# Top-k attention with an MLP mixer on one core: another way to the 32nd largest score, output products in three pieces, other priorities in the plan

## The chip, the cores and the metric

The kernel runs on one core of one Trainium2 chip. The metric is device time in microseconds (us) of one execution, lower is better. A core has five engines that run their own instruction streams and meet at semaphores: PE (matmul), DVE (vector), ACT (activation), POOL (a second elementwise engine) and SP (here it only issues DMAs). All data that the engines work on lies in 128 partitions of on-chip memory; matmul results land in eight PSUM banks.

## The reference

Eight batches, eight heads, 576 rows, head size 64. Each row of scores keeps its 32 largest, and those below are masked; then comes softmax, the product with v, and an MLP mixer over tokens (576 to 256 to 576) and channels (512 to 1536 to 512).

```
scores = scale * np.matmul(q, k.transpose(0, 1, 3, 2))
kth = np.partition(scores, -top_k, axis=-1)[..., -top_k:-top_k + 1]   # top_k = 32
scores = np.where(scores >= kth, scores, -1000000000.0)
attn = np.exp(scores - np.max(scores, axis=-1, keepdims=True))
attn = attn / (np.sum(attn, axis=-1, keepdims=True) + 1e-09)
x = (attn @ v), heads side by side                                     # 8 x 576 x 512
u = x + (np.maximum(x^T @ w_tok1, 0) @ w_tok2)^T
out = u + np.maximum(u @ w_ch1, 0) @ w_ch2
```

## The kernel before

**Units.** The work is cut into 32 units, a pair of heads each (`plan_unit`); four units make a batch, and after each batch come the MLP's channel steps (`plan_mlp`; `plan_mlp_last` for the last batch). A unit has nine row tiles of 128 x 576 scores: tiles 0 to 3 are group 0, tiles 4 to 8 group 1 (tile 8 holds the last 64 rows of both heads).

**From q and k to scores.** SP loads q, k and v (`load_one`); PE transposes q and k (`qk_tr`, L281; `qk_tail_tr`, L296), ACT evacuates them (L291, L304), PE multiplies (`s1_mm` L311, `s0_mm` L334, `st_mm` L353) and ACT copies the scores from PSUM to the tiles SS (L324, L344) and St (L366). There are four SS tiles, one for each group, so two units can be in flight.

**The selection, on DVE.** For each group DVE folds the 576 scores of a row into 288 larger halves of pairs (`upper`, L384), and POOL works out the smaller halves by integer adds (`both_bits` L390, `lower_bits` L399: left + right - larger). `split4` (L407, L411) folds the 288 twice more by max and min. `top_round` (L423, L426) takes the eight largest of growing prefixes of this list four times (MAX8 gives eight values in descending order; MATCH_REPLACE takes them out), and `low_round` (L432) takes the eight largest of the smaller halves. The 40 values lie side by side in A. The first 16 are taken as certain; the 32nd largest is the 16th largest, that is, the eighth smallest, of the next 23. `combine` gets it with MAX8 on negated values:

```
nc.vector.tensor_scalar_mul(X[:, 0:n, :], A[:, 0:n, NR : NA - 1], -1.0)      # L438
for i in range(n):
    nc.vector.max(K[:, i, :], X[:, i, :])                                    # L441
nc.vector.tensor_scalar_mul(kthall[:, c : c + n], K[:, 0:n, 7], -1.0)        # L443
```

The last value of the lists is kept for a test at the end (`keep_ends`, L449, POOL). If that test (L1093 to L1103) finds a row for which the shortened lists were not enough, a slow exact path computes everything again (`full_select`).

**Mask, softmax, product.** ACT takes the exponential (`expo`, L483) with the negated row maximum (`neg_max`, L469, POOL). Tiles 0, 1, 2, 4 and 5 ("turned") are masked first: `raise_kth` (L496, POOL) scales the threshold, ACT makes a large number of all that lies below it (`steep`, L502), POOL subtracts it from the scores (`sink`, L510), and after the exponential a DMA transposes the tile (`turn`, L515). The other tiles are transposed on PE together with their mask (`below_act` L526, `p_tr` L532 and L535, `p_ev` L555, `ptail_tr`, `ptail_ev`). `o_mm` (L601) multiplies with v and a column of ones; there is one PSUM bank O. `o_den` (L613, L614) takes two reciprocals on DVE, one of the four full tiles and one of the 64 rows of the fifth; `o_ev` (L624) scales on ACT.

**MLP.** `h1_mm`, `ut_mm` and their evacuations follow each unit, `h2_mm` (L689) with `h2_ev` (L702) makes the 1536 channels of a batch, and `out_mm` (L711, L715, L719) the output: five row tiles of 15 matmuls each, every tile one task of the plan, in one of the two banks mps. `out_ev` (L731) evacuates, `out_st` stores.

**The order.** Every engine runs its instructions in a written order. `Plan` makes it: each task has an engine, an assumed duration, a priority (100 for each unit, plus an offset; the lowest first), the tasks it needs, and buffers that it takes and gives back. `order` plays this through, and at each free moment starts the ready task with the lowest priority. Where PE is idle in that play, `spare` (L244) puts in matmuls without use that keep PE's clock up. A buffer comes free in the play when the task that releases it ends; for SS, A, nmax and kbig this is a task of no length on POOL with an early priority.

Of the kernel before, what the change touches and what calls it, by code (L numbers as in the profile page):

```python
# [11 lines left out]
LAG = {"PE": 0.11, "ACT": 0.15, "DVE": 0.12, "POOL": 0.06, "SP": 1.2, "DQ": 0.0, "SPQ": 0.0}  # L12
# [3 lines left out]
SPARE = 0.8  # L16
SPARE_US = 0.22
# [7 lines left out]
class Plan:  # L25
# [23 lines left out]
    def order(self):  # L49
# [10 lines left out]
        while left:  # L60
# [13 lines left out]
            for e in free:  # L74
# [14 lines left out]
                if best is not None:  # L89
                    ready[e].remove(best)  # L90
                    if e == "PE" and best.dur > 0.0:
                        at, r, i = min(
# [4 lines left out]
                        )  # L97
# [30 lines left out]
def kernel(  # L128
# [32 lines left out]
    NA = 40  # L161
    NR, NV, NL = 16, 24, 32
# [27 lines left out]
    mgp = pool("mgp", 1)  # L190
# [35 lines left out]
    kthall = const.tile([P, NU * NTILE], f32, tag="kthall")  # L226
    ends = const.tile([P, NU * NTILE, 4], f32, tag="ends")
# [6 lines left out]
    }  # L234
    ctr = {"vb": 0, "pb": 0, "tp": 0, "s0": 0, "O": 0, "mps": 0}
# [180 lines left out]
    def top_round(st, g, r):  # L416
# [5 lines left out]
        for i in range(n):  # L422
            nc.vector.max(A[:, i, 8 * r : 8 * r + 8], hx[:, i, 0:w])  # L423
        if r < 3:
            for i in range(n):
                nc.vector.match_replace(  # L426
                    hx[:, i, 0:w], A[:, i, 8 * r : 8 * r + 8], hx[:, i, 0:w], NEG
                )

    def low_round(st, g):  # L430
        for i in range(4 + g):
            nc.vector.max(st["A", g][:, i, NL:NA], st["lo"][:, i, :])  # L432

    def combine(st, g, u):
        n = 4 + g
        A = st["A", g]
        X = mgp.tile([P, NS, NA - 1 - NR], f32, name="X", tag="X")
        nc.vector.tensor_scalar_mul(X[:, 0:n, :], A[:, 0:n, NR : NA - 1], -1.0)  # L438
        K = mgp.tile([P, NS, 8], f32, name="K", tag="K")
        for i in range(n):  # L440
            nc.vector.max(K[:, i, :], X[:, i, :])  # L441
        c = u * NTILE + 4 * g
        nc.vector.tensor_scalar_mul(kthall[:, c : c + n], K[:, 0:n, 7], -1.0)  # L443
        st["kth", g] = c

    def keep_ends(st, g, u):
        n = 4 + g
        c = u * NTILE + 4 * g
        nc.gpsimd.tensor_copy(out=ends[:, c : c + n, :], in_=st["A", g][:, 0:n, 15:NA:8])  # L449

    def full_select(st, g, u):
        c = u * NTILE + 4 * g
        A = m8p.tile([P, NS, NA], f32, name="A", tag="A")
        R = lists["hi"][:, 0:2, :].rearrange("p a c -> p (a c)")
        for a, i in enumerate(gtiles(g)):
            cur = srow(st, i)
            for r in range(TOPK // 8):
                nc.vector.max(A[:, a, 8 * r : 8 * r + 8], cur)
                if r + 1 < TOPK // 8:
                    nc.vector.match_replace(R, A[:, a, 8 * r : 8 * r + 8], cur, NEG)  # L460
# [727 lines left out]
```

## Time and profile before

| | us |
|---|---|
| median of three runs (1004.16 to 1007.36) | 1005.12 |
| the profiled execution | 1006.08 |
| its span, first to last instruction | 1004.2 |
| busy in the span: PE / DVE / ACT / POOL | 935.5 / 894.6 / 853.5 / 727.9 |
| DVE's first selection instruction starts | 15.18 |
| last threshold (L443) | 943.53 |
| mean granted PE clock | 0.979 |

The busy times are unions on each engine. PE's contains the matmuls without use. The chain that ended last is not of help here: followed back, it stops at the last output copy, so the stages have to be read from stretches and timelines. A group's row gives the line, the engine, the operation, what it writes and reads, how often it runs, its busy time and the mean length of one in ns, and the idle time just before it with what ended it. Lengths of neighbouring instructions overlap by some hundredths of a us, so costs in a row of instructions are read from start to start.

### The profile page before, as it was taken

Reading aid. Unit: us, or ns where it says so; the run is one execution under the profiler, and the core shown is the slowest. Engines: PE = TensorE matmul, PEld = TensorE weight load, DVE = VectorE, ACT = ScalarE, POOL = GpSimd, SP = SyncE. Lnnn points to the kernel's source line nnn. Section 1 sums busy time; section 2 is a strip of 40 time slices with the busy share of each in tenths; the row PEclk is TensorE's granted clock in tenths of the full one; section 3 lists DMA queues with packets and bytes.
Section 4 is the critical chain, followed back from the end, with each engine's and each line's share of the span. In section 5 each row is a group of like instructions: output and inputs, shape, how many; then the busy total and the mean of one; then the engine's idle time right before and its main releaser. Section 6 shows DMA issues by size and latency. Waiting matters only on the chain. (4 is left out here: it accounts for less than half of the span.)

```text
span 1004.2 us, 22286 instructions
## 1 busy us (share of the span) xinstructions
PE 935.5 (93%) x7128; PEld 502.9 (50%) x7128; DVE 894.6 (89%) x4088; ACT 853.5 (85%) x1976; POOL 727.9 (72%) x598
## 2 busy tenths in 40 slices
PE   9889999899999999999999999899999999989995
PEld 6444444455555455454545455454545555444542
DVE  3999999997999979999799979999799997999801
ACT  5667898898999988998999989999899989999731
POOL 3888888886688858888598867888688885888400
PEclk9989899999999999999999999999999999999998
DMA  7454122133332233123322333232233333211201
GB/s 167 120 174 130 38 63 60 45 63 105 68 69 51 69 87 87 40 62 77 81 58 60 80 100 79 45 68 74 66 69 63 75 99 68 46 34 31 71 1 51
DMA packets 229741, 72.65 MB, mean 72 GB/s; under 512 B 222128, under 2 KB 222704, under 8 KB 229616
## 3 DMA queue, kind: packets, MB, share of 16 engines
q1 hardware_dynamic: 229616, 71.15, 29.8%
q8 instruction: 58, 0.95, 0.4%
q14 instruction: 67, 0.55, 0.2%
HBM read 35.78 MB, written 9.44 MB: 45 GB/s over the span
## 5 line engine op out<-in xcount | busy, mean ns | idle before, releaser
L390 POOL TENSOR_TENSOR lo<-SS 128x1152 int32<-128x1152 int32 x64 | 168.4, 2632 | 205.4 <-DVE A L423 188.4
L423 DVE MAX8 A<-hx 128x8 f32<-128x72 f32 (+2 forms) x1152 | 263.0, 288 | 0.0
L510 POOL TENSOR_TENSOR SS<-SS,U 128x576 f32<-128x576 f32 x158 | 199.4, 1280 | 0.0
L426 DVE MATCH_REPLACE8 hx<-A,hx 128x72 f32<-128x72 f32 (+1 forms) x864 | 198.3, 237 | 0.0
L399 POOL TENSOR_TENSOR lo<-lo,hi 128x1152 int32<-128x1152 int32 x64 | 188.0, 2937 | 0.0
L344 ACT COPY SS<-s 128x512 f32<-128x512 f32 x256 | 140.3, 594 | 21.3 <-PE s L334 20.8
L334 PE MATMUL s<-qkT 64*128 64x512 f32 x512 | 154.3, 646 | 0.0
L483 ACT ACTIVATE pb<-SS,nmax 128x576 bf16<-128x576 f32 x158 | 123.0, 786 | 22.0 <-POOL SS L510 21.4
L601 PE MATMUL O<-vb,PT 128*128 128x65 bf16 (+3 forms) x1600 | 122.7, 200 | 10.6 <-ACT Xb L624 10.3
L384 DVE TENSOR_TENSOR hi<-SS 128x1152 f32<-128x1152 f32 x64 | 85.9, 1342 | 49.1 <-ACT SS L344 49.1
L689 PE MATMUL mps<-UT,wc1b 128*128 128x512 bf16 (+1 forms) x768 | 120.7, 292 | 7.2 <-ACT H2T L702 5.2
L502 ACT ACTIVATE U<-SS,kbig 128x576 bf16<-128x576 f32 x158 | 117.4, 786 | 10.4 <-POOL kbig L496 10.2
L601 PEld LDWEIGHTS <-PT 128*128 128x128 bf16 (+3 forms) x1600 | 91.8, 100 | 56.6 <-issue 21.2
L432 DVE MAX8 A<-lo 128x8 f32<-128x288 f32 x288 | 108.3, 434 | 0.0
L532 PE MATMUL tp<-identB,E 128*128 128x128 bf16 (+1 forms) x650 | 98.0, 226 | 9.2 <-ACT PT L555 6.6
L535 PE MATMUL tp<-identN,U 128*128 128x128 bf16 (+1 forms) x650 | 95.6, 223 | 1.9 <-ACT U L526 1.9
L719 PE MATMUL mps<-wc2b,H2T 128*128 128x512 bf16 (+1 forms) x420 | 96.4, 379 | 0.0
L702 ACT ACTIVATE H2T<-mps 128x512 bf16<-128x512 f32 (+1 forms) x180 | 73.2, 430 | 23.4 <-PE mps L689 23.0
L532 PEld LDWEIGHTS <-E 128*128 128x128 bf16 (+1 forms) x650 | 63.9, 101 | 48.1 <-issue 37.5
L689 PEld LDWEIGHTS <-wc1b 128*128 128x128 bf16 x768 | 49.8, 99 | 75.5 <-issue 43.8
L244 PEld LDWEIGHTS <-identB 128*128 128x128 bf16 x650 | 56.5, 103 | 59.0 <-issue 14.8
L624 ACT ACTIVATE Xb<-O,rden 128x64 bf16<-128x64 f32 (+1 forms) x320 | 70.8, 319 | 17.7 <-DVE rden L614 17.3
(100 smaller groups left out, 1760.0 us busy)
## 6 DMA issues: line engine op xcount, KB each, us to landing
qL<-in_q_dram SPq DMA_DIRECT2D x64, 128.0 KB, 2.5
kL<-in_k_dram SPq DMA_DIRECT2D x64, 128.0 KB, 2.5
vL<-in_v_dram SPq DMA_DIRECT2D x64, 128.0 KB, 2.5
out_dram<-ob SPq DMA_DIRECT2D x32, 256.0 KB, 2.1
wst<-in_moe_w_ch_dram SPq DMA_DIRECT2D x4, 1536.0 KB, 7.1
PT<-pb SPq DMA_TRANSPOSE x158, 2.4
qL<-in_q_dram SPq DMA_DIRECT2D x32, 32.0 KB, 2.4
kL<-in_k_dram SPq DMA_DIRECT2D x32, 32.0 KB, 2.3
```

What stands on the lines that cost most here:

```text
L334: nc.tensor.matmul(out=x[:, :], lhsT=T[rows[hh], 0, t * P : (t + 1) * P], rhs=T[rows[hh], 1, 0:W], start=True, stop=True,)
L344: nc.scalar.copy(out=st["SS", t // 2][:, 2 * (t % 2) + hh, 0:W], in_=st["s0", t][hh][:, :])
L390: nc.gpsimd.tensor_tensor(out=x[:, at, :].bitcast(i32), in0=left.bitcast(i32), in1=right.bitcast(i32), op=ALU.add,)
L399: nc.gpsimd.tensor_tensor(out=x, in0=x, in1=st["hi"][:, 0:n, :].bitcast(i32), op=ALU.subtract)
L423: nc.vector.max(A[:, i, 8 * r : 8 * r + 8], hx[:, i, 0:w])
L426: nc.vector.match_replace(hx[:, i, 0:w], A[:, i, 8 * r : 8 * r + 8], hx[:, i, 0:w], NEG)
L483: nc.scalar.activation(out=x, in_=srow(st, i), func=AF.Exp, bias=st["nmax", g][:, a : a + 1], scale=scale,)
L502: nc.scalar.activation(out=U[:, :], in_=srow(st, i), func=AF.Relu, bias=st["kbig", g][:, a : a + 1], scale=-STEEP,)
L510: nc.gpsimd.tensor_tensor(out=x, in0=x, in1=st["U", i][:, :], op=ALU.subtract)
L532: nc.tensor.matmul(out=out, lhsT=st["E", i][:, cols], rhs=identB[:, :], start=True, stop=False)
L601: nc.tensor.matmul(out=O[0:ms, t, :], lhsT=PT[0:kz, hh, j, t * P : t * P + ms], rhs=st["vb"][0:kz, j, hh, :], start=(j == 0), stop=(j == N ...
L689: nc.tensor.matmul(out=ps[:, 0 : hi - lo], lhsT=wc1b[:, cc, fc * P : (fc + 1) * P], rhs=mst["UT"][:, cc, lo:hi], start=(cc == 0), stop=(cc ...
```

## The change

**The threshold.** The values of round 2 and of round 3 (eight each, descending; call them a and b) are paired crosswise, first with last, and the smaller of each pair is taken: one two-input instruction for a group, written between the last but one and the last MAX8 of `low_round`. This gives the eight smaller ones of a and b. One MAX8 for each tile over these eight and the eight of the smaller halves, 16 values, has the threshold as its eighth. No value is negated, X, K and kthall are gone, and the threshold is read from A itself, into whose first round's place it is written. A has 48 columns where it had 40. The test at the end has six comparisons and products where it had three, and `keep_ends` copies five columns where it copied four.

**The reciprocals.** `o_den` is one instruction on all 128 partitions and five columns. The bank O is set to 1 once at the start, so that the rows that are not used hold something.

**Output products.** `out_mm` is three tasks of five matmuls each in place of one of 15, so that other PE work can be ordered between them.

**The plan.** All priorities of the pipeline come from a table RANK; some assumed durations are others; the tasks of no length that give SS, A, nmax and kbig back are on an engine of their own (FREE), and SS and nmax no longer wait for `keep_ends`. Old offsets, for comparison: load -230, vcast -50, qk_tr -160, qk_ev -150, s_mm -140, s_ev -130, st_mm -129, st_ev -119, keep 5, exp_u -50, steep and below -20, sink 0, exp_t -15, p_tr 0, p_ev 20, pt_tr 5, pt_ev 30, o_mm 50, o_ev 30, h1_mm 60, h1_ev -40, ut_mm 61, ut_ev -39, h2_mm 70, h2_ev 0, out_mm 260, out_ev 200.

```diff
+PARTS = 3
+RANK = {
+    "load": -161, "vcast": 25, "qk_tr": -154, "qk_ev": -294, "s_mm": -155, "s_ev": -151, "st_mm": -123, "st_ev": -140,
+    "keep": -1, "exp_u": -41, "steep": 37, "sink": 120, "exp_t": -66, "below": 40, "p_tr": 90, "p_ev": -40,
+    "pt_tr": 95, "pt_ev": 24, "o_mm": 140, "o_ev": 105, "h1_mm": -36, "h1_ev": -40, "ut_mm": 76, "ut_ev": -9,
+    "out_mm": 341, "out_ev": 155, "h2_mm": 28, "h2_ev": 0,
+}
...
-    NA = 40
-    NR, NV, NL = 16, 24, 32
+    NA = 48
+    LO, KTH, TOP = 8, 16, (16, 24, 32, 40)
...
+    nc.vector.memset(banks["O"][0][:, :], 1.0)
...
     def low_round(st, g):
+        n, A = 4 + g, st["A", g]
+        for i in range(n):
+            if i == n - 1:
+                nc.vector.tensor_tensor(
+                    out=A[:, 0:n, 0:8], in0=A[:, 0:n, TOP[2] : TOP[2] + 8],
+                    in1=A[:, 0:n, TOP[3] + 7 : TOP[3] - 1 : -1], op=ALU.min,
+                )
+            nc.vector.max(A[:, i, LO : LO + 8], st["lo"][:, i, :])
+
+    def combine(st, g):
+        A = st["A", g]
         for i in range(4 + g):
-            nc.vector.max(st["A", g][:, i, NL:NA], st["lo"][:, i, :])
-
-    def combine(st, g, u):
-        n = 4 + g
-        A = st["A", g]
-        X = mgp.tile([P, NS, NA - 1 - NR], f32, name="X", tag="X")
-        nc.vector.tensor_scalar_mul(X[:, 0:n, :], A[:, 0:n, NR : NA - 1], -1.0)
-        K = mgp.tile([P, NS, 8], f32, name="K", tag="K")
-        for i in range(n):
-            nc.vector.max(K[:, i, :], X[:, i, :])
-        c = u * NTILE + 4 * g
-        nc.vector.tensor_scalar_mul(kthall[:, c : c + n], K[:, 0:n, 7], -1.0)
-        st["kth", g] = c
+            nc.vector.max(A[:, i, KTH : KTH + 8], A[:, i, 0 : LO + 8])
...
-        nc.vector.reciprocal(rden[:, 0:NT], O[:, 0:NT, D])
-        nc.vector.reciprocal(rden[0:TAIL, NT:NS], O[0:TAIL, NT:NS, D])
+        nc.vector.reciprocal(rden[:, :], O[:, :, D])
...
+        terms = [(identB[0:ss, 0:ss], Xb[0:ss, sc, :])]
+        terms += [(w2b[:, jc, ss_], H1T[:, jc, :]) for jc in range(NJ)]
+        terms += [(H2T[:, fc, ss_], wc2b[:, fc, :]) for fc in range(NF)]
+        n = len(terms)
+        for x in range(part * n // PARTS, (part + 1) * n // PARTS):
             nc.tensor.matmul(
...
-            add("POOL", 0.0, U - 1000, lambda: None, deps=done + [keep[g]],
-                rel=[("SS", u, g), ("A", u, g), ("nmax", u, g)] + ([("St", u)] if g else [])
+            add("FREE", 0.0, 0, lambda: None, deps=done, slack=0.0,
+                rel=[("SS", u, g), ("nmax", u, g)] + ([("St", u)] if g else [])
                 + ([] if fast else [("kbig", u, g)]))
+            add("FREE", 0.0, 0, lambda: None, deps=done + [keep[g]], slack=0.0, rel=[("A", u, g)])
...
+            for part in range(PARTS):
+                done = sc == NS - 1 and part == PARTS - 1
+                a = add("PE", 3.38 / PARTS, M + RANK["out_mm"] + 30 * sc, lambda sc=sc, part=part: out_mm(mst, sc, part),
+                        deps=hs + oms[-1:], acq=[] if part else [("mps", b, "o", sc)],
...
+    for j, (x, op) in enumerate(
+        ((E_1, ALU.is_lt), (E_3, ALU.is_gt), (E_LO, ALU.is_gt), (E_LO, ALU.is_ge), (E_2, ALU.is_lt))
+    ):
+        nc.vector.tensor_tensor(out=FL[:, j, :], in0=x, in1=E_KTH, op=op)
+    nc.vector.tensor_tensor(out=FL[:, 3, :], in0=FL[:, 3, :], in1=FL[:, 4, :], op=ALU.mult)
```

More of the change, by code (lines that the diff above doesn't have):

```diff
@@ L11 @@
 BIG = 3.0e38
-LAG = {"PE": 0.11, "ACT": 0.15, "DVE": 0.12, "POOL": 0.06, "SP": 1.2, "DQ": 0.0, "SPQ": 0.0}
+LAG = {"PE": 0.11, "ACT": 0.15, "DVE": 0.12, "POOL": 0.06, "SP": 1.2, "DQ": 0.0, "SPQ": 0.0, "FREE": 0.0}
 RSLACK = 3.0
@@ L189 @@
     m8p = pool("m8p", 3)
-    mgp = pool("mgp", 1)
     ptp = pool("ptp", 2)
@@ L1154 @@
             for sc in range(NS):
-                out_mm(mst, sc)
+                for part in range(PARTS):
+                    out_mm(mst, sc, part)
                 out_ev(mst, sc)
```

152 lines of the change are left out of this document (71 added, 81 removed).

## The prediction

> **What bounds the kernel now.** First the page's busy times, then the stretches. I cut the span where DVE (the selection) starts, at the two batch boundaries between which five whole batches lie, and at the last threshold. The columns are length, then busy us with the count in brackets for PE, PE's weight loads, DVE, ACT and POOL, then the granted clock and the DMA share.
>
> ```profile
> PE 935.5 (93%) x7128; PEld 502.9 (50%) x7128; DVE 894.6 (89%) x4088; ACT 853.5 (85%) x1976; POOL 727.9 (72%) x598
> ```
>
> ```profile
> 15.20:252.30 237.10, 217.05 (x1567) 114.89 (x1566) 228.71 (x1011) 193.76 (x436) 191.38 (x148) 0.95 0.37 94
> 252.30:833.00 580.70, 552.58 (x4283) 297.92 (x4280) 546.78 (x2540) 533.75 (x1247) 445.34 (x360) 0.99 0.31 71
> 833.00:943.80 110.80, 105.23 (x812) 56.03 (x810) 109.22 (x508) 100.87 (x239) 88.63 (x71) 0.98 0.22 48
> 943.80:1004.20 60.40, 47.20 (x348) 23.05 (x344) 9.90 (x31) 19.42 (x47) 0.27 (x2) 0.94 0.11 32
> ```
>
> The same stretch for PE's matmuls without use (line 244) alone:
>
> ```profile
> 252.30:833.00 580.70, 62.83 (x234) 20.12 (x234) 0.99 0.31 71
> ```
>
> PE is the busiest engine by the page, but 62.8 of its 552.6 us are filling; without them it has 490/5 = 98 us for a batch. A batch of the middle takes 580.7/5 = 116.1 us. In it DVE is busy 546.78/5 = 109.4, ACT 533.75/5 = 106.8, POOL 89. So DVE bounds, and ACT stands only 2.6 us behind it. The reader should keep that pair: it decides what a faster DVE is worth. In the first two batches ACT has less to do (193.8 of 237.1), and in the last 60.4 us there is no selection at all.
>
> The waits of DVE between 253 and 943 us (total, times, longest), and the work around one of them in the timeline:
>
> ```profile
> DVE hi L384 <- ACT SS L344: 33.9, 6, 6.5
> ```
>
> ```profile
> 237.81 2.75 PE L719 MATMUL mps<-wc2b,H2T 128*128 128x512 bf16 x12
> 240.72 0.66 PE L281 MATMUL tp<-identF,kL 128*128 128x128 f32 x4
> ...
> 242.09 2.75 PE L719 MATMUL mps<-wc2b,H2T 128*64 128x512 bf16 x12
> 244.78 0.27 PE L296 MATMUL tp<-identF,qL 64*128 64x64 f32 x1
> ...
> 252.27 1.36 DVE L384 TENSOR_TENSOR hi<-SS 128x1152 f32<-128x1152 f32 x1 [5.06 <-ACT SS L344]
> ```
>
> DVE waits once at each batch boundary, 33.9/6 = 5.65 us each. There the next unit's k is transposed only behind an output product (240.72), and its tail again behind one (244.78); scores and their copies follow, and DVE starts 7 us later. So a batch is 109.4 of DVE work, 5.65 of this hole, and about 1 of gaps.
>
> **The change part by part.** First DVE. The end of one selection and the next group's start, for group 0 (four tiles), a pair of reciprocals, and group 1 (five tiles):
>
> ```profile
> 407.02 1.52 DVE L432 MAX8 A<-lo 128x8 f32<-128x288 f32 x4
> 408.57 0.71 DVE L438 TENSOR_SCALAR X<-A 128x92 f32<-128x92 f32 x1
> 409.32 0.44 DVE L441 MAX8 K<-X 128x8 f32<-128x23 f32 x4
> 409.79 0.25 DVE L443 TENSOR_SCALAR kthall<-K 128x4 f32<-128x4 f32 x1
> 409.94 1.35 DVE L384 TENSOR_TENSOR hi<-SS 128x1152 f32<-128x1152 f32 x1
> ...
> 420.02 0.18 DVE L613 RECIPROCAL rden<-O 128x4 f32<-128x4 f32 x1
> 420.11 0.13 DVE L614 RECIPROCAL rden<-O 64x1 f32<-64x1 f32 x1
> 420.17 1.88 DVE L423 MAX8 A<-hx 128x8 f32<-128x288 f32 x5
> 421.96 1.88 DVE L432 MAX8 A<-lo 128x8 f32<-128x288 f32 x5
> 423.88 0.27 DVE L438 TENSOR_SCALAR X<-A 128x115 f32<-128x115 f32 x1
> 424.18 0.52 DVE L441 MAX8 K<-X 128x8 f32<-128x23 f32 x5
> 424.74 0.26 DVE L443 TENSOR_SCALAR kthall<-K 128x5 f32<-128x5 f32 x1
> 424.91 1.34 DVE L384 TENSOR_TENSOR hi<-SS 128x1152 f32<-128x1152 f32 x1
> ```
>
> ```profile
> L423 DVE MAX8 A<-hx 128x8 f32<-128x72 f32 x576 | 88.6, 215 | 0.0
> L384 DVE TENSOR_TENSOR hi<-SS 128x1152 f32<-128x1152 f32 x64 | 85.9, 1342 | 49.1 <-ACT SS L344 49.1
> L441 DVE MAX8 K<-X 128x8 f32<-128x23 f32 x288 | 30.6, 171 | 2.2
> L438 DVE TENSOR_SCALAR X<-A 128x92 f32<-128x92 f32 x32 | 22.6, 706 | 1.1
> L384 DVE TENSOR_TENSOR hi<-St 128x288 f32<-128x288 f32 x32 | 14.3, 445 | 0.0
> L438 DVE TENSOR_SCALAR X<-A 128x115 f32<-128x115 f32 x32 | 8.7, 272 | 1.0
> ```
>
> - Old tail of a selection: from the end of L432 (408.54 and 423.84) to L384 it is 1.40 and 1.07, 2.47 us for a unit.
> - MAX8 over 16 values: four of 23 take 0.44 and five 0.52, so 0.08 for each after the first. Going from 72 to 23 values saves 44 ns of length (215 to 171), so 16 in place of 23 is worth about 6 ns; I keep 0.08. With the gap of 0.03 ahead, as the old ones have, and 0.08 of overlap with L384, which does not read the threshold, this is 0.35 and 0.43, 0.78 for a unit.
> - The crosswise minimum is in no trace. L384's forms give (1342 - 445)/864 = 1.04 ns for each value, so 32 values last some 0.18 and cost about 0.10 in the row, 0.20 for a unit. Backward reading has no row: if it halved the rate, 32 more ns.
> - Unhindered, a unit saves 2.47 - 0.78 - 0.20 = 1.49, 48 us in 32 units.
> - One reciprocal: the pair holds DVE from 420.02 to 420.17, one alone would to about 420.11: 0.06 times 64 = 4 us.
>
> What may be taken back: L438 has 706 ns for 92 values and 272 for 115. In group 0 it starts inside a POOL `sink` and ends with it; the second pair is a two-input DVE instruction started just behind a POOL cast.
>
> ```profile
> 407.93 1.28 POOL L510 TENSOR_TENSOR SS<-SS,U 128x576 f32<-128x576 f32 x1
> ...
> 59.69 2.82 POOL L781 CAST wc1b<-wst 128x3072 bf16<-128x3072 f32 x1
> 59.94 3.33 DVE L407 TENSOR_TENSOR lo<-hi 128x720 f32<-128x720 f32 x1
> ```
>
> The 0.71 of L438 ends at 409.28, the sink at 409.21; L407 ends 0.76 after the cast. So a two-input instruction can be held, too, and the minimum falls into the time of the sinks. Bounds: 0, and a whole sink, 1.28. I take group 0's own loss, 0.706 - 0.272 = 0.43, once for a unit, since L438 stood at nearly the same place: 14 us, and nothing for group 1. DVE's net gain is 48 + 4 - 14 = 38 us, 1.2 for a unit, 4.7 for a batch: 109.4 becomes 104.7.
>
> The Trainium skill ("SBUF — State Buffer", section "Who interferes with whom") says that a DVE instruction with two SBUF inputs and a POOL instruction that reads SBUF exclude each other for a whole instruction, while a MAX8 with its one input meets nobody. The L407 row agrees. By that rule alone the new minimum is as exposed as the old negation was, and where every one met a sink's start the sum would be that of the third rival.
>
> **What is late next.** ACT. Its 106.8 us for a batch are touched by nothing in the change, and are now above DVE's 104.7. The batch can't go below 106.8; how near it comes is set by the order. ACT idles 116.1 - 106.8 = 9.4 now, 5.65 of it as long as DVE's hole; the remaining 3.75 are small waits. Five matmuls in place of 15 in a task leave a score product at most 1.1 us behind an output product where 3.4 were possible, out_mm stands 81 later and s_mm 15 and s_ev 21 earlier. So I let the hole go, and keep 2.75 of the 3.75, as ACT with a backlog has more to choose from: 109.5 for a batch. PE (98) and POOL (89) stay below. The bounds: 106.8 (no idle), and 115 (hole and small waits both stay on ACT's side).
>
> **Edits with one answer.** The memset of O runs while DVE has nothing (its first selection instruction is at 15.2): 0. `keep_ends` with a fifth column, raise_kth from A: POOL is free a quarter of the time: 0. Loads are ordered 69 later, with unit 0's still first, and a k that has come waits for PE above: 0, at worst one more hole of 5.65 while the weights load. FREE gives buffers back at once in the play where a POOL task had to find a gap: no instruction on the chip, only another order.
>
> The test at the end, on DVE, ahead of a reciprocal:
>
> ```profile
> 946.03 1.84 DVE L1096 TENSOR_TENSOR hi<-ends,kthall 128x288 f32<-128x288 f32 x3
> 947.91 1.05 DVE L1099 TENSOR_REDUCE K<-hi 128x1 f32<-128x864 f32 x1
> 948.88 0.17 DVE L613 RECIPROCAL rden<-O 128x4 f32<-128x4 f32 x1
> ```
>
> Six instructions in place of three at 0.61, and a third more to reduce: 1.84 + 0.3 = 2.1 us before that reciprocal, whose PSUM bank O is the only one. I take 2 us of loss in the last stretch; 0 if the new order puts the reciprocal first.
>
> **The sum**, against the profiled execution:
>
> - Five middle batches: 116.14 to 109.5, 33 us.
> - First two batches: DVE bounds there (228.7 of 237.1). 8 x 1.2 = 9.4 from DVE and the hole of 5.06: 14 us.
> - Last batch: DVE 109.2, less 4.7, ACT at 100.9 below: 5 us.
> - Last stretch: -2 us. Ahead of 15.2: 0.
>
> Span 1004.2 - 33 - 14 - 5 + 2 = 954; the profiled execution has 1006.08 - 1004.2 = 1.9 around it and lies 1 us above the median of the runs, so 955.
>
> **The rivals.**
>
> 1. *ACT fills without a gap.* Middle batches at 106.8 (47 us), the first two lose their small gaps too (17), the minimum is hardly held: 1004.2 - 47 - 17 - 5 + 2 + 1.9 = 939. For it: ACT works 106.8 of 109.4 whenever DVE is not in its hole. Against: one backlog must suit two engines that are equal to 2%.
> 2. *The holes stay.* DVE is shorter but waits at each boundary as before, since ACT, full now, copies the scores late: batch 115, first two 9 gained, last 5, 2 lost: 1004.2 - 6 - 9 - 5 + 2 + 1.9 = 988 at the outside, 980 with half a hole.
> 3. *The minimum waits a whole sink each time.* Unhindered, DVE has 109.4 - 52/8 = 102.9 us a batch; eight minima held for 1.28 make it 113.1, with the gaps of 1 us 114.1 instead of 116.1 (10 us, out of the hole). The first two batches lose 2, the last 4, the last stretch 2: 1004.2 - 10 + 2 + 4 + 2 + 1.9 = 1004, no change. It decides from 0.5 us a piece, where DVE's 102.9 plus eight of them pass ACT's 106.8. For it: L407's row. Against: L438 in group 1 was not held, though a sink ran then, too.
> 4. *Slower: the masking is starved.* steep, sink, below and p_tr now stand 40 to 120 later, behind the next unit's scores, and there are four SS tiles. ACT already waits for sinks (its waits between 252 and 833):
>
> ```profile
> ACT pb L483 <- POOL SS L510: 10.0, 19, 1.2
> ```
>
> If late sinks hold SS, the next scores can't be copied, and DVE waits in every unit and not in every fourth. The gains outside the middle are 17 us; the middle loses them again at 119.6 a batch, that is with ACT idle for 12.9, or 3.2 a unit where 2.3 are idle now. With 5 a unit it would be 127 and 1041 us. Against: sinks have POOL a quarter free, and the play of the plan counts the SS tiles.
>
> **How the numbers follow.** Forecast 955 (945 to 975): 0.58. Rival 1, 0.15; rival 2, 0.15; rival 3, 0.02; rival 4, 0.10. The range 935 to 988 takes in the forecast, most of rival 1 and most of rival 2, and leaves out 2 in 10. A measurement here tells a change from none at 0.3%, 3 us: faster 0.88, same 0.02, slower 0.10.
>
> **What the profile after would show.** Right: no L438 and L443; from the end of L432 to L384 0.35 to 0.45; the minimum below 0.7 on average, long where a POOL sink runs; DVE near 104.7 a batch; the DVE waits for L344 gone or below 2 us each; ACT over 96% in the middle; the last stretch near 62. Wrong: minima above 1 us (rival 3), the 5 us waits still there (rival 2), DVE waiting for ACT in every unit (rival 4), or ACT's own busy time changed, which I hold fixed.

## The result, and the profile after

The change made the kernel slower: 1019.8 us (median of 4 runs, 1016.45 to 1021.47) against 1006.1 for the kernel before in the same comparison, a ratio of 1.0133 with an interval of 1.0101 to 1.0166. The prediction was 955. The profiled execution after has a span of 1019.7.

Busy times, and the same four stretches as before (first selection instruction, two batch boundaries with five batches between them, last threshold, end), with the same columns:

```profile
PE 916.9 (90%) x6869; PEld 495.9 (49%) x6869; DVE 939.0 (92%) x3964; ACT 852.5 (84%) x1976; POOL 776.3 (76%) x598
```

```profile
15.60:252.00 236.40, 211.00 (x1493) 109.38 (x1491) 235.66 (x981) 192.45 (x432) 197.44 (x147) 0.95 0.37 93
252.00:826.70 574.70, 528.78 (x4044) 289.70 (x4042) 571.53 (x2461) 523.84 (x1232) 474.55 (x358) 0.96 0.31 71
826.70:945.30 118.60, 106.43 (x826) 57.10 (x825) 118.43 (x494) 106.48 (x247) 100.55 (x74) 0.97 0.20 49
945.30:1019.70 74.40, 56.79 (x385) 28.24 (x383) 12.90 (x32) 23.97 (x59) 1.46 (x2) 0.87 0.10 30
```

DVE ran 124 instructions fewer and was busy 44 us longer. In the middle it was busy 571.5 of 574.7 us: no hole is left, and each batch takes 114.9 us because DVE's own work takes 114.3, where it had been 109.4. The waits for the scores, which held the holes, have one row, and 14.2 of its 16.4 us are the start of the kernel:

```profile
DVE hi L391 <- ACT SS L351: 16.4, 3, 14.2
```

What became longer is one kind of instruction. DVE's groups after, two-input ones and, for comparison, the new MAX8 and the new reciprocal:

```profile
L391 DVE TENSOR_TENSOR hi<-SS 128x1152 f32<-128x1152 f32 x64 | 92.2, 1440 | 16.4 <-ACT SS L351 16.4
...
L414 DVE TENSOR_TENSOR hx<-hi 128x720 f32<-128x720 f32 x32 | 52.2, 1631 | 0.0
L418 DVE TENSOR_TENSOR hx<-lo 128x360 f32<-128x360 f32 x64 | 43.1, 712 | 0.0
L441 DVE TENSOR_TENSOR A<-A 128x32 f32<-128x32 f32 x32 | 36.2, 1132 | 0.0
L414 DVE TENSOR_TENSOR hx<-hi 128x576 f32<-128x576 f32 x32 | 34.5, 1080 | 0.0
...
L450 DVE MAX8 A<-A 128x8 f32<-128x16 f32 x288 | 26.7, 153 | 0.0
...
L441 DVE TENSOR_TENSOR A<-A 128x40 f32<-128x40 f32 x32 | 18.0, 563 | 0.0
...
L621 DVE RECIPROCAL rden<-O 128x5 f32<-128x5 f32 x64 | 11.5, 180 | 16.9 <-PE O L609 16.9
```

The same instructions of the kernel before (L407 is L414 after, L411 is L418):

```profile
L411 DVE TENSOR_TENSOR hx<-lo 128x360 f32<-128x360 f32 x64 | 31.0, 525 | 0.0
...
L407 DVE TENSOR_TENSOR hx<-hi 128x720 f32<-128x720 f32 x32 | 28.8, 900 | 0.0
L407 DVE TENSOR_TENSOR hx<-hi 128x576 f32<-128x576 f32 x32 | 24.3, 760 | 0.0
```

The minimum (L441) of 32 and 40 values lasts 1.13 and 0.56 us. And the folds that the change does not touch are longer: all forms of `upper` and `split4` together took 273.5 us before and 325.3 after. From here on "folds" means that sum, and "threshold instruction" the minimum, or, in the old way, the L438 negation (31.3 us before; the minimum is 54.2 after). MAX8, with one input, is nearly as long as it was (the MAX8 of `top_round` 291 ns, 288 before).

The timeline shows who holds whom. DVE and then POOL of the kernel after, around one group's end:

```profile
402.57 1.16 DVE L445 MAX8 A<-lo 128x8 f32<-128x288 f32 x3
403.65 1.17 DVE L441 TENSOR_TENSOR A<-A 128x32 f32<-128x32 f32 x1
404.75 0.45 DVE L445 MAX8 A<-lo 128x8 f32<-128x288 f32 x1
405.12 0.17 DVE L621 RECIPROCAL rden<-O 128x5 f32<-128x5 f32 x1
405.21 0.36 DVE L450 MAX8 A<-A 128x8 f32<-128x16 f32 x4
405.49 1.33 DVE L391 TENSOR_TENSOR hi<-SS 128x1152 f32<-128x1152 f32 x1
...
435.11 0.91 DVE L414 TENSOR_TENSOR lo<-hi 128x720 f32<-128x720 f32 x1
435.93 1.31 DVE L414 TENSOR_TENSOR hx<-hi 128x720 f32<-128x720 f32 x1
```

```profile
402.26 2.51 POOL L518 TENSOR_TENSOR SS<-SS,U 128x576 f32<-128x576 f32 x2
...
435.22 1.26 POOL L280 CAST vb<-vL 128x512 bf16<-128x512 f32 x1
436.43 0.96 POOL L281 CAST vb<-vL 64x128 bf16<-64x128 f32 x1
```

Two sinks of POOL end at 404.77, and the minimum ends at 404.82. The minimum came 0.15 us after the second of them had started. At 435 the two engines hold each other in turn: the cast of v comes 0.11 us behind the first instruction of `split4`, and takes 1.26 where its mean was 0.61 before; the second instruction of `split4` stands behind that cast, and takes 1.31 where its mean was 0.90; the small cast is next. In the new order the casts lie there, and in the mean they became longer themselves:

```profile
L280 POOL CAST vb<-vL 128x512 bf16<-128x512 f32 x32 | 36.2, 1130 | 1.0
L281 POOL CAST vb<-vL 64x128 bf16<-64x128 f32 x32 | 23.7, 739 | 0.0
```

Before, the larger cast had:

```profile
L273 POOL CAST vb<-vL 128x512 bf16<-128x512 f32 x32 | 19.6, 613 | 0.0
```

So a DVE instruction with two inputs and a POOL instruction that is under way with it are not done side by side. The Trainium skill ("SBUF — State Buffer", section "Who interferes with whom") says that a DVE instruction with two SBUF inputs contends with a POOL instruction that reads SBUF, that the port pair is an exclusive lock, and that the order of issue decides who is blocked; this trace agrees, with 1.13 us for a minimum that lasts 0.17 to 0.19 where no sink runs (shown below).

How much of this is whose can be counted. In the trace after, every fold and minimum that lasts over 0.03 us longer than the shortest of its form starts while a POOL instruction is under way. What they last too long sums to 62.3 us for the folds (sinks 38.1, casts of v 16.7, casts of weights 7.5) and 43.1 for the minimum (sinks 40.3). In the kernel before it is 9.9 for the folds, all of it beside the four large casts of weights: no fold was held by a sink or by a cast of v.

The rest of the loss is at the end. The last MAX8 of the threshold starts at 944.86, only 1.3 us later than the last threshold instruction before (943.53), but the last stretch is 74.4 us in place of 60.4.

### The profile page after: what moved, and what is told of

Read it like the earlier page. It is cut to its first block, busy times and chain, and to the rows that moved or that the text cites. A ratio compares the mean times of both kernels' runs of the same rounds, so it can differ in the third digit from the quotient of the medians.

```text
span 1019.7 us, 21660 instructions
## 1 busy us (share of the span) xinstructions
PE 916.9 (90%) x6869; PEld 495.9 (49%) x6869; DVE 939.0 (92%) x3964; ACT 852.5 (84%) x1976; POOL 776.3 (76%) x598
## 5 line engine op out<-in xcount | busy, mean ns | idle before, releaser
L518 POOL TENSOR_TENSOR SS<-SS,U 128x576 f32<-128x576 f32 x158 | 214.6, 1378 | 11.2 <-ACT U L510 9.7
L341 PE MATMUL s<-qkT 64*128 64x512 f32 x512 | 172.6, 674 | 4.4 <-ACT SS L331 4.2
L504 POOL TENSOR_SCALAR kbig<-A 128x4 f32<-128x4 f32 (+1 forms) x63 | 88.5, 1405 | 50.0 <-DVE A L450 47.6
L540 PE MATMUL tp<-identB,E 128*128 128x128 bf16 (+1 forms) x650 | 102.9, 229 | 18.5 <-ACT PT L563 7.5
L445 DVE MAX8 A<-lo 128x8 f32<-128x288 f32 x288 | 114.5, 443 | 0.2
L543 PE MATMUL tp<-identN,U 128*128 128x128 bf16 (+1 forms) x650 | 100.2, 227 | 14.0 <-ACT U L534 9.2
L725 PE MATMUL mps<-wc2b,H2T 128*128 128x512 bf16 (+1 forms) x420 | 108.4, 389 | 0.0
L391 DVE TENSOR_TENSOR hi<-SS 128x1152 f32<-128x1152 f32 x64 | 92.2, 1440 | 16.4 <-ACT SS L351 16.4
L696 PEld LDWEIGHTS <-wc1b 128*128 128x128 bf16 x768 | 54.8, 99 | 88.3 <-issue 47.4
L543 PEld LDWEIGHTS <-U 128*128 128x128 bf16 (+1 forms) x650 | 67.0, 104 | 47.7 <-issue 24.6
```

The costliest lines, as they stand in the source:

```text
L341: nc.tensor.matmul(out=x[:, :], lhsT=T[rows[hh], 0, t * P : (t + 1) * P], rhs=T[rows[hh], 1, 0:W], start=True, stop=True,)
L518: nc.gpsimd.tensor_tensor(out=x, in0=x, in1=st["U", i][:, :], op=ALU.subtract)
L543: nc.tensor.matmul(out=out, lhsT=st["U", i][:, cols], rhs=identN[:, :], start=False, stop=True)
L696: nc.tensor.matmul(out=ps[:, 0 : hi - lo], lhsT=wc1b[:, cc, fc * P : (fc + 1) * P], rhs=mst["UT"][:, cc, lo:hi], start=(cc == 0), stop=(cc ...
```

## The experiments

All ratios are to the kernel before, timed beside it. "Middle batch" is a fifth of the time between the two batch boundaries. "Red" in a label stands for the minimum made by a reduction.

### Threshold or plan?

The kernel before with the new threshold alone (its plan, two reciprocals and tasks of 15 products stay), and the kernel after with the old threshold (its plan, pieces and single reciprocal stay):

```diff
 before to b_thr (and, the other way round, after to a_oldthr)
-        nc.vector.tensor_scalar_mul(X[:, 0:n, :], A[:, 0:n, NR : NA - 1], -1.0)
-            nc.vector.max(K[:, i, :], X[:, i, :])
-        nc.vector.tensor_scalar_mul(kthall[:, c : c + n], K[:, 0:n, 7], -1.0)
+                nc.vector.tensor_tensor(out=A[:, 0:n, 0:8], ..., op=ALU.min)
+            nc.vector.max(A[:, i, KTH : KTH + 8], A[:, i, 0 : LO + 8])
```

> The kernel before with the new threshold alone (old reciprocals, old output products, old order and plan). Theory A (the crosswise minimum, a two-input DVE instruction, is held by POOL's instruction that is under way, about as long as the threshold saves): the minimum measures 0.4 to 1.1 us in the mean against 0.17 at its shortest, the tail of a selection stays near 2.4 us a unit, time 1000 to 1010. Rival B (the new order is what costs; the threshold is worth its 1.5 us a unit): 960 to 980, minima below 0.3 us.

> The changed kernel with the old threshold (negations, K, kthall, three comparisons at the end); order, pieces and the one reciprocal are the new ones, the plan's durations too. Theory A: the new minimum and its holds cost what the negations cost, so DVE's work hardly changes, and the other holds (the folds of split4 beside POOL's sinks and casts) stay: 1010 to 1025. Rival B: the same or worse, 1015 to 1060, with DVE waiting for scores. Were the threshold itself the loss: below 1000.

Measured: b_thr 1003.53 us (0.9959, 0.9939 to 0.9979), folds 281.4, minimum 50.8. a_oldthr 1016.67 us (1.0106, 1.0086 to 1.0126), folds 316.4, threshold instruction 32.6, waits of DVE for scores 13.5 us, once. So the threshold by itself is a small gain, not the 48 us that it removes from the row, because its minimum is held even in the old order:

```profile
L432 DVE TENSOR_TENSOR A<-A 128x32 f32<-128x32 f32 x32 | 37.4, 1167 | 0.0
```

And everything but the threshold, the plan above all, is a loss of about 10 us although it closes the holes: with the old threshold the folds are 43 us longer than before. The two findings of the profile after, held minimum and held folds, are two causes.

a_oldthr also shows that one of the old negations was never a measure of the hold. That of 92 values (group 0) is held as in the kernel before (748 ns). That of 115 values (group 1) takes 0.27 us wherever it stands, here 0.63 us into a sink that runs until 76.30:

```profile
75.65 0.27 DVE L447 TENSOR_SCALAR X<-A 128x115 f32<-128x115 f32 x1
```

```profile
75.02 1.28 POOL L519 TENSOR_TENSOR SS<-SS,U 128x576 f32<-128x576 f32 x1
```

Why the one form is held and the other not, no run here shows.

### The minimum with one input

A reduction reads one operand, so the pairs can be brought side by side: round 2 is written backwards into A, and a reduction over two rows of eight takes the minimum. Nothing is added; the test at the end becomes a little stricter.

```diff
-            nc.vector.max(A[:, i, TOP[r] : TOP[r] + 8], hx[:, i, 0:w])
+            o = A[:, i, TOP[r] + 7 : TOP[r] - 1 : -1] if r == 2 else A[:, i, TOP[r] : TOP[r] + 8]
+            nc.vector.max(o, hx[:, i, 0:w])
...
-                nc.vector.tensor_tensor(...)
+                two = A[:, 0:n, TOP[2] : TOP[3] + 8].rearrange("p n (t e) -> p n e t", t=2)
+                nc.vector.tensor_reduce(out=A[:, 0:n, 0:8], in_=two, op=ALU.min, axis=AX.X)
```

> The changed kernel, but the crosswise minimum is made by a one-input reduction over pairs (round 2's list is written backwards for it), in the same place of the same order. Theory A: the minimum takes 0.15 to 0.25 us whatever POOL does, 1.45 us a unit go from DVE, and with ACT next the time is 980 to 995. Rival B: the order decides, DVE's shorter work turns into waits for scores, 1010 to 1020.

> The kernel before, its own order, with the new threshold whose minimum is the one-input reduction; nothing else. Theory A: DVE loses the negations' 1.5 us a unit and no minimum is held; a part of the hold moves to the next group's first instruction, as in the changed kernel with the reduction (its L391 rose from 1440 to 1649 ns there): 972 to 988 us, with the waits of 5 to 6 us at the batch boundaries still there. Rival B (only the order matters): 1000 to 1006.

> The same with the one reciprocal and three comparisons at the end (any row whose smaller halves reach the threshold goes to the slow path). 4 us from 64 second reciprocals if DVE bounds in the stretches between the holes: 968 to 985, and 2 to 5 below the run without them.

Measured: a_red 984.09 us (0.9785, 0.9765 to 0.9804), 36 us less than the kernel after, as expected, but ACT did not come next: a middle batch is still DVE's (552.3 busy of 553.3 us in five). b_red, the kernel before with this threshold, 995.76 us (0.9899, 0.9879 to 0.992), with folds up from 273.5 to 303.8: a miss, since 972 to 988 were expected. b_redr, which adds the single reciprocal and a test of three comparisons to b_red, 996.8 us (0.9921, 0.9902 to 0.994): a miss too. The 4 us that the reciprocal takes from DVE's row are not seen in the time; its folds are 3.6 us longer than b_red's (307.4).

The reduction is never held: over a_red's 64 it takes 0.19 to 0.22 us. The groups of a_red, and a piece of its DVE and POOL timelines:

```profile
L391 DVE TENSOR_TENSOR hi<-SS 128x1152 f32<-128x1152 f32 x64 | 105.5, 1649 | 12.9 <-ACT SS L351 12.9
...
L443 DVE TENSOR_REDUCE A<-A 128x40 f32<-128x80 f32 x32 | 6.9, 216 | 0.0
L443 DVE TENSOR_REDUCE A<-A 128x32 f32<-128x64 f32 x32 | 6.5, 202 | 0.0
```

```profile
431.63 0.22 DVE L443 TENSOR_REDUCE A<-A 128x40 f32<-128x80 f32 x1
...
432.14 0.46 DVE L451 MAX8 A<-A 128x8 f32<-128x16 f32 x5
432.52 2.19 DVE L391 TENSOR_TENSOR hi<-SS 128x1152 f32<-128x1152 f32 x1
```

```profile
429.74 3.76 POOL L519 TENSOR_TENSOR SS<-SS,U 128x576 f32<-128x576 f32 x3
```

The reduction takes its 0.22 us in the midst of three sinks. But the next instruction with two inputs, `upper` (L391), starts at 432.52 with the third sink still running until 433.50, and takes 2.19 where 1.33 is its length: it is held for about what was left. Over the kernel, L391 goes from 1440 to 1649 ns. So a hold that is taken from one instruction is in part handed to the next. In b_red longer folds eat most of the gain: `upper` goes from 1462 in b_thr to

```profile
L382 DVE TENSOR_TENSOR hi<-SS 128x1152 f32<-128x1152 f32 x64 | 103.1, 1611 | 52.9 <-ACT SS L342 52.9
...
L382 DVE TENSOR_TENSOR hi<-St 128x288 f32<-128x288 f32 x32 | 27.0, 845 | 0.0
```

and the small form from 446 to 845 ns. The small form is not held by a sink but by the cast of v: with the shorter selection this cast meets the large `upper`, is held by it (615 ns in b_thr, 1708 in b_red), and then holds the small one. So the old written order, too, gets new holds when only the selection becomes shorter.

### No sinks

The most direct test: the kernel after with its two-input minimum, but without POOL's subtraction. The scores of the turned tiles are then not masked, and softmax runs over all 576 of them; the work of the other engines stays.

```diff
-        nc.gpsimd.tensor_tensor(out=x, in0=x, in1=st["U", i][:, :], op=ALU.subtract)
+        pass
```

> The changed kernel without the subtraction on POOL (the scores of the turned tiles are not masked, so their softmax runs over all 576 scores); every other instruction and the whole order stay. Theory A (POOL's subtractions hold the minimum and the folds): the minimum falls from 1132 and 563 ns to below 250 in both forms, the folds from 325 us to 270 to 290 (the casts of v and of the weights stay), DVE's busy time from 939 to 830 to 860, time 945 to 985. Rival C (the minimum is long of itself, by its backward reading or by waiting for the MAX8 just ahead): it stays above 500 ns.

Measured: 936.82 us (0.9315, 0.9295 to 0.9336), below the 945 to 985 expected, with a middle batch of 104.64. Both minima have their own length (0.17 to 0.19 us; the mean of 223 contains one of 1.73, beside a cast of weights), and `upper` has the 1.34 of the profile before:

```profile
L391 DVE TENSOR_TENSOR hi<-SS 128x1152 f32<-128x1152 f32 x64 | 85.7, 1340 | 13.3 <-ACT SS L351 13.3
...
L441 DVE TENSOR_TENSOR A<-A 128x32 f32<-128x32 f32 x32 | 7.1, 223 | 0.0
L441 DVE TENSOR_TENSOR A<-A 128x40 f32<-128x40 f32 x32 | 5.7, 178 | 0.0
```

That shows that the sinks hold the minimum and `upper`. Of the folds' 325.3 us, 287.9 are left; the remaining excess over before is mostly in `split4`'s 720 form, which stands beside the casts of v (1341 ns, 900 before). The run also takes a chain of waits away (ACT's exponentials no longer wait for sinks), so not all of the 83 us between it and the kernel after need be holds: the minimum became 41 us shorter and the folds 37, and DVE's busy time falls by 80 (939.0 to 858.7).

### Which priority puts POOL's work there?

First, casts back to their old place (vcast 25 to -50), alone; all 28 old offsets at once, with new durations, FREE and pieces kept; and the old offsets of the masking chain and the casts only (vcast, steep, sink, exp_t, below, keep).

```diff
 a_vcast
-    "vcast": 25
+    "vcast": -50
 a_oldrank: RANK = the old offsets, all of them
 a_pool: RANK's vcast -50, steep -20, sink 0, exp_t -15, below -20, keep 5
```

> The changed kernel with the offset of the cast of v back from 25 to -50, nothing else. In the changed kernel the folds of group 1 (128x720) run 1.00 and 1.63 us where 0.91 and 0.90 are their unheld lengths, and POOL's two casts of v lie beside them. Theory A (these folds are held by the casts): the two forms fall to about 0.95 each, up to 26 us go from DVE, 995 to 1008 us. Rival (POOL's sinks take the place of the casts beside the folds): the forms stay above 1.2 and the time is 1014 to 1022.

> The changed kernel with all offsets of the priorities as before; the threshold, the one reciprocal, the pieces, the new assumed durations and FREE stay. The folds and their first instruction (upper and split4) sum to 273 us in the kernel before and 325 in the changed one, where their shortest lengths give 262. Theory A1 (the new offsets put POOL's sinks and casts beside the folds): the sum falls below 285, time 995 to 1006. Rival A2 (the new durations and FREE, or the shorter selection itself, shift POOL's work as much): the sum stays above 300, time 1008 to 1030.

> The changed kernel with the old offsets for the masking chain alone (v's cast, steep, sink, the turned exponentials, below_act, keep_ends). Theory A1 in its narrow form (the later sinks are what lies beside the folds): the folds' sum falls from 325 to below 290, time 980 to 1000. Rival A2: above 305, time 1010 to 1030.

Measured:

| | time, us | ratio | folds, us | minimum, us | waits for scores, us (times) |
|---|---|---|---|---|---|
| after | 1019.8 | 1.0133 (1.0101 to 1.0166) | 325.3 | 54.2 | 16.4 (3) |
| a_vcast | 1027.39 | 1.0199 (1.0168 to 1.0231) | 331.5 | 61.2 | 15.0 (3) |
| a_oldrank | 1028.52 | 1.0230 (1.0201 to 1.0258) | 296.5 | 51.4 | 66.8 (16) |
| a_pool | 990.67 | 0.9851 (0.9832 to 0.9870) | 309.6 | 46.4 | 16.7 (4) |

a_vcast was a miss for the theory that the casts are the cause. The casts themselves were free again (621 ns), but sinks took their place beside DVE: the minimum of group 0 rose from 1132 to 1407 ns and `split4`'s 576 form from 1080 to 1215. Counted as above, the casts of v hold no fold there, and the sinks hold the folds for 58.4 us (38.1 in the kernel after).

a_oldrank shows that the offsets are not the whole of it: with all the old ones the folds are still 23 us above the kernel before, 20.7 of them beside the casts of v, and the holes are back, more of them. a_pool, six offsets together, was 29 us faster than the kernel after, a time as expected, but its folds did not fall below 290: they gave some 16 of the 29, the minimum 8, and the last stretch most of the rest. Of the six only vcast was tried alone, and that lost some 7. Which of durations, FREE and offsets places POOL's work where is open.

### The output products

```diff
 a_parts1
-PARTS = 3
+PARTS = 1
 a_out
-    "out_mm": 341
+    "out_mm": 260
```

> The changed kernel with each output product in one task again, its priority still the new one. If the pieces are what took away DVE's waits of 5.65 us at the batch boundaries: waits of 3 to 6 us come back, some 20 to 30 us in all, and the time is 1025 to 1045. If the priorities did it: no such waits, 1015 to 1024.

> The changed kernel with out_mm's offset back from 341 to 260. If the output products that were put off into the last stretch are part of its 14 us: there are fewer of them behind the last threshold, h2 starts 3 to 8 us sooner after it (32.3 us now), 1011 to 1017. If not: 1018 to 1022. Holes at the batch boundaries may come back and cost up to 15 us more.

Measured: a_parts1 1014.46 us (1.0063, 1.0036 to 1.0090), 18.9 us of waits for scores in 3 times; a_out 1034.72 us (1.0274, 1.0240 to 1.0308), 22.5 us in 5 times. With whole tasks of 15 the holes stay nearly gone (one wait of 4.0 us behind the start), and with out_mm at its old offset they come back in part. So it was the priorities that removed the holes (a_oldrank, with the pieces and the old offsets, has them), and the three pieces are not needed for it; here they even cost some 5 us. a_out was a miss: its time was lost in the folds (340.1), which the expectation held still, so it does not tell what out_mm itself is worth. Nor did it empty the last stretch: 33 matmuls of output products stand behind the last threshold there, 25 in the kernel after.

### The last stretch

In the kernel after, DVE has this order behind the last threshold:

```profile
944.86 0.46 DVE L450 MAX8 A<-A 128x8 f32<-128x16 f32 x5
945.63 4.08 DVE L1105 TENSOR_TENSOR hi<-ends 128x288 f32<-128x288 f32 x5 [0.32 <-POOL ends L455]
...
951.51 1.80 DVE L527 TENSOR_SCALAR U<-SS,A 128x576 bf16<-128x576 f32 x4
...
977.18 0.23 DVE L1051 TENSOR_SCALAR H2T<-mps 128x64 bf16<-128x64 f32 x1 [5.91 <-PE mps L696]
```

Before, the masks of the last group came right behind the threshold:

```profile
943.84 1.84 DVE L519 TENSOR_SCALAR U<-SS,kthall 128x576 bf16<-128x576 f32 x4
...
962.14 0.22 DVE L1045 TENSOR_SCALAR H2T<-mps 128x64 bf16<-128x64 f32 x1 [5.17 <-PE mps L689]
```

The whole loss lies ahead of the first H2T evacuation: from there to the end it is 42.5 after (1019.7 - 977.18) and 42.1 before. The experiment makes the test's comparisons, its product and its reduction tasks of the plan behind the last reciprocal:

```diff
-    FL = lists["hi"] ... compare, multiply, reduce      (outside the plan; it ran ahead of the last masks)
+    x = add("DVE", 0.6, 10**6, compare, deps=[last o_den]) ... add("DVE", 1.4, 10**6, any_flag, deps=[x])
```

> The changed kernel with the closing test's comparisons written behind the last reciprocal in the plan, no longer ahead of the last group's masks. If the test in front of the masks is what makes the last stretch 14 us longer: h2 starts 6 to 12 us earlier after the last threshold, time 1008 to 1014. If the left-over output products and PE's lower clock there make it: 1017 to 1020.

Measured: 1013.43 us (1.0068, 1.0046 to 1.0090), 6.4 us less than the kernel after.

```profile
944.74 0.46 DVE L450 MAX8 A<-A 128x8 f32<-128x16 f32 x5
...
945.21 2.79 DVE L527 TENSOR_SCALAR U<-SS,A 128x576 bf16<-128x576 f32 x4
...
969.53 0.23 DVE L1052 TENSOR_SCALAR H2T<-mps 128x64 bf16<-128x64 f32 x1 [1.11 <-PE mps L696]
```

From the last MAX8 to that evacuation it is 24.8 us in place of 32.3; before, from the last threshold instruction, 18.6. So the test in front of the masks costs 7.5 of some 13.7. The three stretches, before, after and a_late:

```profile
943.53:962.14 18.61, 17.55 (x186) 11.39 (x186) 5.95 (x16) 10.72 (x33) 0.54 (x3) 1.00 0.16 35
```

```profile
944.86:977.18 32.32, 27.32 (x224) 16.62 (x224) 9.12 (x22) 15.66 (x46) 1.46 (x2) 0.84 0.11 29
```

```profile
944.74:969.53 24.79, 23.35 (x222) 14.28 (x224) 9.00 (x22) 15.20 (x46) 1.99 (x2) 1.00 0.15 38
```

The second column is PE's busy time, the last but two its granted clock. PE fills most of each stretch. After, it waits once for the masks (4.36 us, ending at 952.08), and is busy for 27.3 us at a clock of 0.84 with about the work that takes 23.4 in a_late, at 1.00. These two make up the 7.5 (a_late has a wait of 0.6 elsewhere). The 6.2 us that are left in a_late are not the clock, which is 1.00 in both. There PE is 5.8 us longer busy than before, and output products that are left over take 6.2 us (24 matmuls of L725), where before one of 0.4 was left. That is read from the traces; no run took these products out of the stretch alone.

### Put together

The reduction, the late test cut to three comparisons (c_rl), then with the casts' old offset (c_rlv), then with the masking chain's old offsets as in a_pool (d_best):

```diff
 c_rl = a_red + a_late + test of 3 comparisons
 c_rlv = c_rl, "vcast": -50
 d_best = c_rl, "vcast": -50, "steep": -20, "sink": 0, "exp_t": -15, "below": -20, "keep": 5
```

> Three repairs together on the changed kernel: the minimum as a one-input reduction, the closing test behind the last reciprocal and cut to three comparisons (the minimum of round 2 is no longer kept apart, so any row whose smaller halves reach the threshold goes to the slow path), and the cast of v at -50. Theory A, all holds that are named gone: the reduction alone gave 984; the test 7 less, the casts up to 26 less, ACT at 106.8 us a batch sets a floor: 952 to 972. Rival B (the order is the loss): not below 980.

> The changed kernel with the minimum as a reduction and the closing test late and short, v's cast left at 25. If the two repairs add up, 984 less 7: 975 to 980. If the 1004 of the run with v's cast moved too came from the test and not from the cast's new place: above 995.

> The last with the masking chain's old offsets as well (v's cast, steep, sink, turned exponentials, below_act, keep_ends: 990.7 with the held minimum). If holds can be removed one by one: 950 to 970. If a hold that is removed in one place comes back at the next two-input instruction, as from the minimum to upper: 970 to 988, with folds above 310 us.

Measured: c_rl 982.87 us (0.9776, 0.9761 to 0.9791), c_rlv 1004.11 us (0.9965, 0.9950 to 0.9981), d_best 965.17 us (0.9612, 0.9599 to 0.9626). c_rl missed its range by 3 us: the late test adds some 1 us to what a_red gained, not 7. In a_red the test stands ahead of the masks as well, but PE waits there only 1.0 us for them, and its granted clock between the last MAX8 and the first H2T evacuation is 0.90, in c_rl 0.91. c_rlv was a clear miss: one priority costs about 20 us, folds 335.7 to 353.4, with the same instructions on DVE, ACT and POOL; the casts of v hold nothing there, and the sinks hold the folds for 79.5 us in place of 49.3. d_best beats both kernels, by 40 us the one before. Its time is that of gains which add up, its folds (316.0) those of holds that move: the middle batch of 109.4 is DVE's (541.9 busy of 546.9), and it still has about 43 us of holds in the folds against the kernel before.

## Why the prediction was wrong

**What was right.** DVE bounds, and the holes at the batch boundaries went (33.9 us to 2.2 behind the start). L438 and L443 are gone, and the end of a selection runs as forecast: from the end of the last `low_round` MAX8 (405.20) to L391 (405.49) it is 0.29 us, forecast 0.35, with a reciprocal inside. The single reciprocal takes 0.09 us in the row, as assumed, though no run shows its 4 us in the time. DVE's forecast batch of 104.7 agrees with d_nosink, where no sink holds anything (104.64), but in part by luck: the forecast holds 1.7 us a batch for the minimum, which d_nosink does not have, and has nothing for the casts of v, which hold folds there for 16.8 us over the kernel, some 2 a batch.

**The step that failed: "what may be taken back".** It took 0.43 us for a unit, from L438's own loss, in group 0 alone, and 0 for group 1. With the 0.20 of the minimum itself that is 20 us; 54.2 were measured, 34 more. L438 was no measure, for two reasons. In group 0 the place is not the same: the minimum is written ahead of the last MAX8, L438 stood behind it. So in the old order, too (b_thr), most of the minima start 0.11 to 0.31 us into a sink, where L438 started 0.6 to 0.8 us into it, and both end with that sink: 1167 ns where the negation had 706. Whether the minimum behind the last MAX8 would wait less, no run tried. In group 1 the negation of 115 values is a form that is not held (a_oldthr, 0.27 us in the midst of a sink), and its row said nothing of the minimum, which took 418 ns there in b_thr and 563 in the kernel after. The row nearest to the right size was there, the 1.28 of a sink, and the text used it as a bound only.

**The step that is missing: the folds.** Their lengths were held fixed. They are two-input instructions as well, eleven in a unit, and with the change sinks and casts of v hold them (38.1 and 16.7 us, nothing before; casts of weights 7.5, 9.9 before): +52 us. Neither the sum nor a rival had a term for it. Together the two are 86 us of DVE's length; DVE's busy time came out 80 above the forecast (939.0 against 894.6 - 38 + 2).

**Rival 3 was the right mechanism, at the wrong size.** "The minimum waits a whole sink each time" got a chance of 0.02, against it the L438 of group 1 that was not held, though a sink ran; as just said, that form is held nowhere. Its threshold of 0.5 us for a piece was passed in both groups. But with the minimum alone it ended at no change, 1004; the folds make it 1019.8. The rule of the Trainium skill that the prediction names ("SBUF — State Buffer", section "Who interferes with whom") covers every DVE instruction with two SBUF inputs beside a POOL instruction that reads SBUF. The traces agree (62.3 us in the folds after), and it should have been applied to every moved POOL task.

**ACT as the next bound.** It was never reached in the change itself: ACT was busy 523.8/5 = 104.8 us of a batch of 114.9. Nor was 106.8 a floor: with the same ACT instructions d_nosink has middle batches of 104.64, with 514.6/5 = 102.9 of ACT in them. The stretch that gave 106.8 holds 1247 ACT instructions, the one after 1232, so a percent of it was work of a neighbouring batch.

**The last stretch, +2.** It was +14. The test was costed by its length ahead of a reciprocal; it went ahead of the last group's masks, from which transposes, products and the last MLP hang, and that was 7.5, of which PE's own wait is 4.4. The output products left over there are nearly all of the rest, and had no term.

Where the 65 us between forecast and result lie: five middle batches 27 (114.9 against 109.5), the first two batches 13 (236.4 against 223.1), the last 13 (118.6 against 105.8), the last stretch 12 (74.4 against 62.4). DVE's lengths, with the folds taken as fixed, make up the first three; the place of the test makes up more than half of the fourth, the output products left over most of its rest.

## What to carry to other kernels

Before a two-input DVE instruction is added, or POOL work is moved, list which POOL instructions can be under way at each of the two-input DVE instructions, and price every one of them with the rest of a POOL instruction, not with its own length. A one-input instruction that a trace shows held (here the negation of 92 values) belongs on the list, and one form's row does not speak for another's. Where a form with one input does the same (a reduction over pairs in place of a minimum of two operands: 0.2 us in place of 1.13), it escapes, but look at once at the next two-input instruction, which gets part of the hold. A written order that leaves such holds out of its play does not foresee them: the same DVE, ACT and POOL instructions ran in 983 or 1004 us with one priority changed. A play that counts them was not tried.

## What was not expected of the hardware

- A reduction over 64 or 80 values takes 0.20 to 0.22 us, in the midst of sinks too, while a minimum of 32 values with two inputs took 1.13 on average in the kernel after. The Trainium skill ("SBUF — State Buffer", section "Who interferes with whom") says that a reduction on this chip never contends with POOL; a_red agrees, with 216 and 202 ns.
- POOL is held as DVE is: the cast of 128x512 went from 613 to 1130 ns, and from 292 to 739 the small one, where the order put them beside `split4`. `raise_kth` comes right behind the threshold and so meets `upper`: at 405.65 it takes POOL 1.25 us, until 406.91, beside the `upper` of 405.49 to 406.82. On average it takes 1.59 us for 128x4 values (1.25 before), where `neg_max`, the same operation on as many values, takes 0.23.
- The place inside a POOL instruction makes the price: in the kernel after, most minima of group 0 start 0.12 to 0.24 us into a sink of 1.28 and last 1.08 to 1.21; those of group 1 that are held mostly start 0.61 to 0.75 us into it and last 0.58 to 0.72. With three sinks in a row from 429.74 to 433.50 in a_red, `upper` at 432.52 was held for 0.86 us, by the last of them.
- Where one sink follows another at once, a held instruction may go in between or wait for both. In the kernel after, 23 of 24 go in between: the minimum of 57.01 ends at 57.33 although the next sink runs from 57.25. But the minimum of 572.29 took 1.98 us, through the rest of one sink and the whole of the next, and in a_vcast 17 of the 32 minima of group 0 took 1.89 to 2.01. What decides it is not shown.
- PE's granted clock over the span was 0.952 after and 0.979 before. What that is worth over the span no run separates; behind the last threshold it is 0.84 after and 1.00 in a_late, and the same transposes (L543, 128x128) take 283 ns there and 219.
